# The head of an attention and gated-MLP kernel: one transfer for masks and identity in front, then q and k of the first pair, and half of the filling matmuls

## Chip, cores and metric

One Trainium2 chip, one core. The metric is the device time of one execution in microseconds (us). The kernel before takes 509.92 us (median of 3 runs, 509.29 to 510.59).

## What is computed

Eight batches of 576 tokens. Attention has 8 heads of 64; the first four see a local band of 32 keys, the other four the keys whose position is congruent to the query's modulo 32. Its output, 576 x 512 for a batch, goes through a gated layer with a product over the sequence.

```python
scores = scale * np.matmul(q, k.transpose(0, 1, 3, 2))
mask_local = (rel >= 0) & (rel < stride)
mask_strided = (rel >= 0) & (pos[None, :] % stride == pos[:, None] % stride)
scores = np.where(masks[None, :, :, :], scores, -1000000000.0)
attn = softmax(scores);  x = attn @ v        # heads side by side
h = np.maximum(x @ w_in, 0.0)                # 512 -> 1024
u, v = h[..., :512], h[..., 512:]
v_n = (v - mean(v)) / np.sqrt(var(v) + 1e-06)
v_s = np.einsum('ts,bsd->btd', w_spatial, v_n) + b_spatial[None, :, None]
return ((u * v_s) @ w_out).astype(np.float32)
```

## The kernel before

Heads are worked on in pairs: a batch has two local pairs (`t` modulo 4 is 0 or 1) and two strided ones (2 or 3), 32 pairs in all. A pair is loaded (`q`; `k` of a local pair, or two pieces of `kbd` of a strided one; `v`), its scores are made on TensorE (line 486 local, line 629 strided), maxima, exponentials, sums and a transposition follow on VectorE and ScalarE, the transposed weights are copied into `ptl` or `pts` by ScalarE and GpSimd (lines 391 and 393), and TensorE makes the product with v (line 596 local, line 700 strided). The result `x` (line 413 and 401) feeds the products with w_in (lines 961 and 1018), the product over the sequence (line 1099) and the one with w_out (line 1149). Weights come in blocks by DMA as well and are converted on the way (`convert`, lines 781 to 797), in the first 50 us.

No engine's order is written by hand. Every step is added to a `Program` with a key, a cost for each engine that may do it, and what it reads and writes; `Program.order` simulates the engines and takes from what is ready the step with the smallest key; `Program.emit` issues the steps in that order. All transfers are issued by SyncE (lines 420 and 1290 for loads, 1180 for results), in one queue, the keys of the first ones being `KEYS["la"]`, `KEYS["lb"]`, `KEYS["cst"]` and such. The pairs of the first batch are worked on in the order 0, 2, 1, 3: in the rows below, "the first pair" is `t` = 0 (local), "the third" `t` = 2 (strided), "the second" `t` = 1 (local), "the fourth" `t` = 3 (strided).

For the first four pairs the mask is put into PSUM by TensorE ahead of the scores (`mask_scores`, line 460): minus the identity times minus the mask. Both come by DMA (`cst`, three masks of 64 columns, line 1290; `eye`, the identity, line 1292, into a buffer of the ring of outputs), and ScalarE multiplies them by -1 (lines 1294, 1299 and 1300).

Where TensorE would stand idle in the simulation, `Program.fillers` puts matmuls of zeros ahead of a step: into the PSUM bank that the step is going to overwrite, 256 columns each, as many as fit into a share of the gap (`WARM_SHARE`; line 1378 issues them):

```python
gap = at - max([free, 600.0, *(ends[m] + 200.0 for m in before)])
if gap > WARM_GAP:
    found[n] = int(WARM_SHARE * gap / WARM_COST)
```

Of the kernel before, what the change touches and what calls it, by code (L numbers as in the profile page):

```python
# [9 lines left out]
F32 = mybir.dt.float32  # L10
# [8 lines left out]
B, H, S, D = 8, 8, 576, 64  # L19
# [15 lines left out]
SP = S + STRIDE - RA  # L35
NU = 2 * SB
HS = S // 2
TAIL = S - 4 * P
NT = 4
KEYS = {  # L40
    "a": (-4467.57, -3072.23, -4097.95, -922.09, -62.58, 1948.86, -54.07, 1313.94,),
# [18 lines left out]
    "la": (-2830.09, -2292.21, -5019.65, -1683.98, -4639.4, -3037.2, 298.54, 1600.86,),  # L60
    "lb": (-1002.76, 2105.75, -428.93, 3194.59, 1811.71, 608.19, -588.14, 3548.95,),
}
WARM_END, WARM_GAP, WARM_COST, WARM_COLS, WARM_SHARE = 110000.0, 700.0, 427.0, 256, 0.8
PE_MASKED, APART = (0, 1, 2, 3), ()
OTHER_BANK = (1, 2, 3)
FETCHED, FETCH_COST = 100.0, 32.0
DMA_RATE, DMA_ISSUE, DMA_LAG, DMA_TAIL = 405.0, 475.0, 1600.0, 900.0
# [10 lines left out]
PE, ACT, DVE, POOL, DMA = "tensor", "scalar", "vector", "gpsimd", "sync"  # L78
# [69 lines left out]
class Program:  # L148
# [2 lines left out]

    def __init__(self):
        self.ops, self.writer, self.readers, self.spare = [], {}, {}, {}
        self.tiled, self.port, self.kind = {}, {}, {}

    def add(self, key, choices, fn, reads=(), writes=(), spare=None, tiled=0, port=(), kind=0):


        n = len(self.ops)
        if port:  # L160
            self.port[n] = port
        self.kind[n] = kind
        if spare is not None:
            self.spare[n] = spare
        if tiled:
            self.tiled[n] = tiled
        deps = set()
        for tok in reads:
            if tok in self.writer:
                deps.add(self.writer[tok])  # L170
            self.readers.setdefault(tok, []).append(n)
        for tok in writes:
            if tok in self.writer:
                deps.add(self.writer[tok])
# [139 lines left out]
    def emit(self, nc, warm):  # L314
        issued = self.order()
        fillers = self.fillers(issued)
        for _, n, e in issued:
            if e == PE and fillers.get(n):
                warm(self.spare[n][1], fillers[n])
            self.ops[n][2](getattr(nc, e))  # L320
# [8 lines left out]


@with_exitstack
def attention_moe(ctx, tc, qT, kT, ks, vl, vs, cst, eye, w_in, w_out, wsp, wtail, out):
    nc = tc.nc
    nb = qT.shape[0]

    sb = ctx.enter_context(tc.tile_pool(name="sb", bufs=1))
    ps = ctx.enter_context(tc.tile_pool(name="ps", bufs=1, space=PSUM))
    prog = Program()
    add = prog.add
# [1 line left out]
    def f32(t):  # L341
        return t.bitcast(F32)

    cst_sb = sb.tile([P, 3, 2 * STRIDE], F32, name="cst_sb")
    mask_l0, mask_l, mask_s = cst_sb[:, 0], cst_sb[:, 1], cst_sb[:, 2, :RA]
    w_in_sb = sb.tile([P, 2, NT, DFF], F32R, name="w_in_sb")
    wsp_sb = sb.tile([P, 2, NT, S], F32R, name="wsp_sb")
    wt_h = sb.tile([P, S], F32R, name="wt_h")
# [23 lines left out]
    r_wo = Ring(sb, "w_out", [P, 2, 2, len(BLOCKS), DM // 2], F32R, 1)  # L372
    r_bn = Ring(sb, "bn", [P, 12], F32, 3)
    r_o = Ring(sb, "o", [P, HS], F32, 4)
    at_raw, at_minus = r_o.new(), r_o.new()
    minus = lambda: at_minus()[:, :P].bitcast(F32R)
    masks = lambda i, k: at_minus()[:, P + 2 * STRIDE * i : P + 2 * STRIDE * i + k].bitcast(F32R)
    r_ps = Ring(ps, "s", [P, 512], F32, 2)
# [37 lines left out]

        add(key, [(e, cost[e]) for e in engs], fn, reads, writes)

    def load(key, dst, src, writes, nbytes, reads=()):
        add(key, [(DMA, nbytes / DMA_RATE)], lambda eng: eng.dma_start(dst(), src), reads, writes)  # L420

    xs = {}

# [298 lines left out]
    def attention(t, due):  # L722
        b, hp = divmod(t, NHP)
        local = hp < 2
        q, k = r_q.new(), None
        if t == 2:
            place = r_xt.new()
            v = lambda: f32(place()).rearrange("p a b c -> p (a b c)").rearrange("p (u d) -> p u d", d=D)
        else:
            v = place = r_v.new()  # L730
        fetch_k, fetch_v = (KEYS[n][t] if t < len(KEYS[n]) else due - d for n, d in (("la", 33), ("lb", 20)))
        load(fetch_k - 1, q, qT[b, hp], [(q,)], P * SP * 4)
        if local:
            k = r_k.new()
            load(fetch_k, k, kT[b, hp], [(k,)], P * (STRIDE + S) * 4)
            load(fetch_v, lambda: v()[:, : 2 * LB, :], vl[b, hp], [(place,)], P * 768 * 4)
            kin = [(k,)]
        else:
            for j in range(2):
                load(  # L740
                    fetch_k, lambda j=j: kbd[j::2, t % 2, j, STRIDE:],
                    ks[b, hp - 2, j], [("k", t % 2, j)], 64 * S * 4, [("k0", t % 2)],
                )
            load(fetch_v, v, vs[b, hp - 2], [(place,)], P * 1024 * 4)
            kin = [("k", t % 2, j) for j in range(2)]
        (local_attention if local else strided_attention)(t, due, q, k, v, [(place,)], kin)
# [291 lines left out]
    def keep_tails(bs, key):  # L1038
        xt = r_xt.new()
        xtl[bs[0]] = xt  # L1040
        for i, b in enumerate(bs):
            for hp in range(NHP):
                t = NHP * b + hp
                rnd(
                    key, 2 * TAIL,
                    lambda hp=hp, i=i: xt()[:, hp, :, TAIL * i : TAIL * i + TAIL],
                    lambda t=t: f32(xs[t]())[:, :, 4 * P :],
# [213 lines left out]
    lead = min(nb, 2)  # L1261
# [23 lines left out]
    if nb <= lead:  # L1285
# [1 line left out]
    when, units = zip(*knots)  # L1287
    when = [w - KEYS["lead"][0] for w in when]

    add(KEYS["cst"][0], [(DMA, 330)], lambda eng: eng.dma_start(cst_sb, cst), (), [("cst",)])  # L1290

    load(KEYS["cst"][0] + 1, lambda: at_raw()[:, :P], eye, [(at_raw,)], P * P * 4)
    add(
        KEYS["cst"][0] + 2, [(ACT, 200)], lambda eng: eng.mul(minus(), at_raw()[:, :P], -1.0),
        [(at_raw,)], [(at_minus,)],
    )

    def turn_masks(eng):
        eng.mul(masks(0, 4 * STRIDE), cst_sb[:, :2].rearrange("p a k -> p (a k)"), -1.0)
        eng.mul(masks(2, RA), mask_s, -1.0)  # L1300

    add(
# [84 lines left out]
def _layout(q, k, v, w_in, w_spatial, b_spatial, w_out):  # L1387
    nb = q.shape[0]
    r_major = np.arange(S).reshape(RA, STRIDE).T.reshape(-1)

    def heads(x, width, first):
        xt = np.concatenate([x[:, : H // 2], x[:, H // 2 :][:, :, r_major]], axis=1)
        out = np.zeros((nb, NHP, P, width), np.float32)
        out[..., first : first + S] = xt.transpose(0, 1, 3, 2).reshape(nb, NHP, P, S)
        strided = out[:, NHP // 2 :].reshape(nb, NHP // 2, 2, D, width)
        out[:, NHP // 2 :] = strided.transpose(0, 1, 3, 2, 4).reshape(nb, NHP // 2, P, width)
        return out

    qT, kT = heads(q, SP, 0), heads(k, STRIDE + S, STRIDE)
    ks = kT[:, NHP // 2 :, :, STRIDE:].reshape(nb, NHP // 2, D, 2, S).transpose(0, 1, 3, 2, 4)  # L1400
    vpad = np.zeros((nb, H // 2, S + 32, D), np.float32)
    vpad[:, :, 32:] = v[:, : H // 2]
    vl = np.stack([vpad[:, :, LQ * c : LQ * c + LK] for c in range(LB)], axis=2)
    vl = vl.reshape(nb, 2, 2, LB, LK, D).transpose(0, 1, 4, 3, 2, 5)
    vl = np.ascontiguousarray(vl).reshape(nb, 2, P, 2 * LB, D)
    vsp = v[:, H // 2 :][:, :, r_major].reshape(nb, 2, 2, STRIDE, RA, D)
    vsp = vsp[:, :, :, [[strided_residue(c, i) for i in range(4)] for c in range(SB)]]
    vs = np.zeros((nb, 2, 4, STRIDE, SB, 2, D), np.float32)
    vs[:, :, :, :RA] = vsp.transpose(0, 1, 4, 5, 3, 2, 6)
    vs = vs.reshape(nb, 2, P, NU, D)  # L1410

    cst = np.zeros((P, 3, 2 * STRIDE), np.float32)
    i = np.arange(STRIDE)[:, None]
    j = np.arange(2 * STRIDE)[None, :]
    band = np.where((j > i) & (j <= i + STRIDE), 0.0, NEG)
    cst[:, :2] = np.tile(band, (4, 1))[:, None]
    cst[:STRIDE, 0] += np.where(j < STRIDE, NEG, 0.0)
    cst[:, 2] = np.tile(np.where((j > i) & (i < RA), NEG, 0.0), (4, 1))

    def words(w):  # L1420
        w = np.ascontiguousarray(w)
        return w.view(np.int64) if w.dtype == np.float64 else w

    wspT = np.ascontiguousarray(w_spatial.T)
    wtail = np.zeros((2, P, S), np.float32)
    wtail[0, :TAIL] = wspT[4 * P :]
    wtail[0, TAIL:] = wspT[4 * P :]
    wtail[1, :TAIL] = wspT[4 * P :]
    wtail[1, TAIL] = wtail[1, 96] = b_spatial
    return {  # L1430
        "qT": qT,
        "kT": np.ascontiguousarray(kT[:, : NHP // 2]),
        "ks": np.ascontiguousarray(ks),
        "vl": vl,
        "vs": vs,
        "cst": cst,
        "eye": np.eye(P, dtype=np.float32),
        "w_in": words(w_in.reshape(NT, P, 2, HF).transpose(0, 2, 1, 3)),
        "w_out": words(w_out),
        "wsp": wspT[: 4 * P],  # L1440
        "wtail": wtail,
    }
# [19 lines left out]
```

## Time and profile before

| | |
|---|---|
| median of 3 runs | 509.92 us (509.29 to 510.59) |
| the profiled execution | 509.85 us, of it span 507.8 us |
| TensorE (PE) busy | 495.6 us, 98% of the span |
| VectorE (DVE), ScalarE (ACT), GpSimd (POOL) busy | 344.7, 280.3, 111.7 us |
| DMA | 52.71 MB, 104 GB/s on average |
| mean granted TensorE clock | 0.99 of full speed |

A matmul in float32 shows up as two records. The profile calls weight loads PEld and the sync queue's issues SPq. "Granted clock" is the share of full speed (2.4 GHz) that TensorE was given; a DMA's time to landing counts from the start of its issue. The chain of waits follows back from the last instruction what released each step.

### The profile page before, as it was taken

What the parts mean: (1) busy time and instruction counts of PE and PEld (TensorE: products, weight loads), DVE (VectorE), ACT (ScalarE), POOL (GpSimd) and SP (SyncE); (2) the same over time, 40 slices, a digit from 0 to 9 for tenths busy, and PEclk for the clock granted to TensorE, in tenths of its full rate; (3) what the DMA queues carried; (4) which work ended last, traced back from release to release, by engine and by line L of the source; (5) the groups of instructions that cost most, each with busy time, mean ns of one, the idle gap of its engine ahead of it and who ended that gap; (6) DMA issues with size and microseconds to landing.
All of it is one profiled execution on the core that took longest, in us unless ns stands there. A gap on an engine that the chain in (4) does not pass through costs nothing.

```text
span 507.8 us, 15733 instructions
## 1 busy us (share of the span) xinstructions
PE 495.6 (98%) x6398; PEld 455.2 (90%) x6398; DVE 344.7 (68%) x1069; ACT 280.3 (55%) x871; POOL 111.7 (22%) x229
## 2 busy tenths in 40 slices
PE   7599999999999999999999999999999999999997
PEld 4478898889988999899998999989998899989997
DVE  3988898988678628784488925687288841666055
ACT  5897777577546556373654765355554642235214
POOL 3553426133232013020221211121022200120000
PEclk9699999999999999999999999999999999999999
DMA  8996443422423412204224243024131020002002
GB/s 288 397 359 222 125 139 108 137 93 64 144 92 119 127 50 91 90 25 151 81 92 138 76 132 89 4 90 139 60 99 45 1 94 0 1 2 93 1 1 94
DMA packets 26247, 52.71 MB, mean 104 GB/s; under 512 B 3136, under 2 KB 11584, under 8 KB 26176
## 3 DMA queue, kind: packets, MB, share of 16 engines
q1 hardware_dynamic: 26176, 51.72, 31.0%
q8 instruction: 50, 0.82, 0.7%
q14 instruction: 21, 0.17, 0.1%
HBM read 42.27 MB, written 9.44 MB: 102 GB/s over the span
## 4 chain that ended last, share of the span: by engine, by line
PE 95%; DMA 4%; SPq 0%; issue 0%; ACT 0%
PE m L961 21%; PE m L1018 20%; PE m L1099 20%; PE m L1149 18%; PE po L700 3%; PE po L596 3%; DMA q<-qT 3%; PE s L486 2%; PE s L629 2%; PE m L1111 2%; PE m L1112 2%; DMA kbd<-ks 1%; PE po L1378 0%; SPq L420 0%; PE m L629 0%
## 5 line engine op out<-in xcount | busy, mean ns | idle before, releaser
L1099 PE MATMUL m<-wsp_sb,vn 128*128 128x288 f32 x768 | 112.9, 296 | 0.0
L1099 PEld LDWEIGHTS m<-wsp_sb,vn 128*128 128x128 f32 x768 | 105.5, 189 | 0.9
L1018 PE MATMUL m<-x,w_in_sb 128*128 128x288 f32 x768 | 105.3, 297 | 0.0
L1018 PEld LDWEIGHTS m<-x,w_in_sb 128*128 128x128 f32 x768 | 103.0, 188 | 0.6
L961 PE MATMUL m<-w_in_sb,x 128*128 128x512 f32 (+1 forms) x408 | 99.4, 398 | 0.0
L1149 PE MATMUL m<-g,w_out 128*128 128x288 f32 x672 | 92.9, 296 | 0.0
L1149 PEld LDWEIGHTS m<-g,w_out 128*128 128x128 f32 x672 | 89.9, 188 | 1.3
L961 PEld LDWEIGHTS m<-w_in_sb,x 128*128 128x128 f32 (+1 forms) x408 | 74.1, 185 | 18.3
L393 POOL TENSOR_SCALAR ptl<-pc 32x64 f32<-32x64 f32 (+3 forms) x98 | 38.5, 393 | 105.5 <-DVE pc L567 69.5
L916 DVE BATCH_NORM_STATS2 bn<-vv 128x6 f32<-128x512 f32 (+1 forms) x37 | 25.2, 683 | 47.4 <-ACT vv L911 47.1
L391 ACT CAST g<-u 128x288 fp32r<-128x288 f32 x91 | 39.0, 435 | 29.4 <-DVE u L812 13.1
L543 ACT ACTIVATE pl<-pl,ml 128x64 f32<-128x64 f32 (+1 forms) x140 | 47.0, 337 | 7.9 <-DVE ml L523 7.8
L929 POOL TENSOR_TENSOR bn<-bn,sel 128x1 f32<-128x1 f32 (+1 forms) x37 | 21.5, 582 | 130.0 <-DVE bn L924 125.2
L401 DVE TENSOR_TENSOR g<-u,g 128x288 fp32r<-128x288 f32 x98 | 43.6, 459 | 7.5 <-ACT g L391 5.2
L911 ACT ACTIVATE vv<-m 128x512 f32<-128x512 f32 (+1 forms) x37 | 21.9, 596 | 47.0 <-PE m L961 46.7
L1032 ACT ACTIVATE u<-m 128x288 f32<-128x288 f32 x56 | 22.9, 409 | 41.2 <-PE m L1018 40.5
L1121 DVE TENSOR_TENSOR u<-m,u 128x288 f32<-128x288 f32 x56 | 24.9, 453 | 30.5 <-PE m L1112 29.9
L391 ACT COPY ptl<-pc 32x320 f32<-32x320 f32 (+3 forms) x94 | 33.5, 356 | 13.7 <-DVE pc L567 11.9
L413 ACT CAST x<-po 128x288 fp32r<-128x288 f32 x60 | 22.1, 399 | 22.2 <-PE po L700 10.3
L401 DVE TENSOR_TENSOR x<-po,x 128x288 fp32r<-128x288 f32 x64 | 27.3, 447 | 8.4 <-ACT x L413 7.9
L523 DVE CUSTOM_DVE_ANT_0 pl<-s,cst_sb 128x64 f32<-128x64 f32 (+1 forms) x140 | 22.1, 215 | 14.5 <-PE s L486 14.5
L543 ACT ACTIVATION_READ_ACCUMULATOR pl<-pl,ml 128x1 f32 (+1 forms) x140 | 26.3, 188 | 0.0
(128 smaller groups left out, 632.8 us busy)
## 6 DMA issues: line engine op xcount, KB each, us to landing
q<-qT SPq DMA_DIRECT2D x32, 295.0 KB, 4.3
v_raw<-vs SPq DMA_DIRECT2D x15, 512.0 KB, 3.8
v_raw<-vl SPq DMA_DIRECT2D x16, 384.0 KB, 3.7
k<-kT SPq DMA_DIRECT2D x16, 304.0 KB, 4.5
kbd<-ks SPq DMA_DIRECT2D x32, 144.0 KB, 4.9
outT<-o SPq DMA_DIRECT2D x32, 144.0 KB, 1.9
outT<-u SPq DMA_DIRECT2D x28, 144.0 KB, 1.8
vn<-w_in SPq DMA_DIRECT2D x4, 512.0 KB, 7.5
```

Source lines behind the costliest of these rows:

```text
L391: eng.copy(dst(), src())
L393: eng.tensor_scalar(dst(), src(), 1.0, 0.0, op0=ALU.mult, op1=ALU.add)
L401: eng.tensor_tensor(dst(), src(), f32(hi()), op=ALU.subtract)
L413: eng.copy(dst(), src())
L543: eng.activation(p_sb()[:m, u, :], src, AF.Exp, bias=st()[:m, u : u + 1], scale=SCALE if masked else -1.0, **total,)
L916: lambda eng: eng.bn_stats(bn()[:m, 0:6], v()[:m]), [(v,)], [(bn,)],
L961: eng.matmul(v_ps()[:m, :], x_at(kt)[:, a, :], w_in_sb[:, w, kt, HF:], start=(n == 0 and i == 0), stop=(n == NT - 1 and i == 2),)
L1018: eng.matmul(u_ps()[:, :HS], w_in_sb[:, w, kt, f * P : (f + 1) * P], xs[NHP * b + kt]()[:, a, r], start=(n == 0 and i == 0), stop=(n == NT ...
L1032: lambda eng, u=u, f=f, u_ps=u_ps: eng.activation(flat(u)[:, f * HS : (f + 1) * HS], u_ps()[:, :HS], AF.Relu),
L1099: eng.matmul(s_ps()[:, :HS], vn()[:, a, kt, fs], wsp_sb[:, w, kt, r], start=(kt == 0 and i == 0), stop=False,)
L1121: lambda eng, ug=ug, s_ps=s_ps: eng.tensor_tensor(ug(), s_ps()[:, :HS], ug(), op=ALU.mult),
L1149: eng.matmul(o_ps()[:, :HS], w_out_t[0]()[:, w, r, BLOCKS[name], j * P : (j + 1) * P], at(a), start=(first and r == 0 and i == 0), stop=(r ...
```

## The change

- The masks and the identity lie side by side in one array `cst` of 274 columns (137 KB), `cst_sb` holds it, and one DMA brings it; `eye`, its DMA and its buffer are gone. The step of the identity remains in the program as one that issues nothing.
- Steps can have a `lead`; `emit` issues those ahead of everything else, in the order of their numbers: `cst` (0), q of the first pair (1), k of the first pair (2). The simulated order is made without regard to it.
- `WARM_SHARE` is 0.4 instead of 0.8.

```diff
-WARM_END, WARM_GAP, WARM_COST, WARM_COLS, WARM_SHARE = 110000.0, 700.0, 427.0, 256, 0.8
+WARM_END, WARM_GAP, WARM_COST, WARM_COLS, WARM_SHARE = 110000.0, 700.0, 427.0, 256, 0.4
...
+        if lead is not None:
+            self.lead[n] = lead
...
     def emit(self, nc, warm):
         issued = self.order()
         fillers = self.fillers(issued)
+        for n in sorted(self.lead, key=self.lead.get):
+            self.ops[n][2](getattr(nc, DMA))
         for _, n, e in issued:
+            if n in self.lead:
+                continue
...
-    cst_sb = sb.tile([P, 3, 2 * STRIDE], F32, name="cst_sb")
-    mask_l0, mask_l, mask_s = cst_sb[:, 0], cst_sb[:, 1], cst_sb[:, 2, :RA]
+    cst_sb = sb.tile([P, CST], F32, name="cst_sb")
+    mask_l0, mask_l = cst_sb[:, : 2 * STRIDE], cst_sb[:, 2 * STRIDE : 4 * STRIDE]
+    mask_s, one = cst_sb[:, 4 * STRIDE : 4 * STRIDE + RA], cst_sb[:, CST - P :]
...
-        load(fetch_k - 1, q, qT[b, hp], [(q,)], P * SP * 4)
+        load(fetch_k - 1, q, qT[b, hp], [(q,)], P * SP * 4, lead={0: 1}.get(t))
...
-            load(fetch_k, k, kT[b, hp], [(k,)], P * (STRIDE + S) * 4)
+            load(fetch_k, k, kT[b, hp], [(k,)], P * (STRIDE + S) * 4, lead={0: 2}.get(t))
...
-    add(KEYS["cst"][0], [(DMA, 330)], lambda eng: eng.dma_start(cst_sb, cst), (), [("cst",)])
-    load(KEYS["cst"][0] + 1, lambda: at_raw()[:, :P], eye, [(at_raw,)], P * P * 4)
+    add(KEYS["cst"][0], [(DMA, 330)], lambda eng: eng.dma_start(cst_sb, cst), (), [("cst",)], lead=0)
+    add(KEYS["cst"][0] + 1, [(DMA, P * P * 4 / DMA_RATE)], lambda eng: None, (), [("one",)])
     add(
-        KEYS["cst"][0] + 2, [(ACT, 200)], lambda eng: eng.mul(minus(), at_raw()[:, :P], -1.0),
-        [(at_raw,)], [(at_minus,)],
+        KEYS["cst"][0] + 2, [(ACT, 200)], lambda eng: eng.mul(minus(), one, -1.0),
+        [("one",)], [(at_minus,)],
     )
```

How the instructions stand now. On VectorE, ScalarE and GpSimd every instruction keeps its place; on the other two, the rows below are all that differs. First the sync queue at the start of the program, before:

```order
L420 DMA q_1_83<-qT 128x590
L1290 DMA cst_sb_61<-cst 128x192
L420 DMA o_0_91<-eye 128x128
L420 DMA q_0_97<-qT 128x590
L420 DMA k_0_100<-kT 128x608
L420 DMA vn_0_103<-w_in 128x1024
L420 DMA kbd_68<-ks 64x576 x2
```

and now (`q_0` and `k_0` are the first pair's, `q_1` the third's, `vn_0` holds the first block of w_in):

```order
L1301 DMA cst_sb_61<-cst 128x274
L429 DMA q_0_82<-qT 128x590
L429 DMA k_0_84<-kT 128x608
L429 DMA q_1_88<-qT 128x590
L429 DMA vn_0_101<-w_in 128x1024
L429 DMA kbd_68<-ks 64x576 x2
```

The masks moved from second to first, the first pair's q and k from fourth and fifth to second and third, the third pair's q from first to fourth; all that follows stands one place further ahead. Then TensorE, where the filling matmuls stand (those of `zeros`), before:

```order
L1378 MATMUL s_0_116<-zeros_67 32x256 x8
L460 MATMUL s_0_116<-o_1_110 128x64
...
L1378 MATMUL po_0_337<-zeros_67 32x256
L596 MATMUL po_0_337<-ptl_72,v_raw_0_182 64x96 x6
...
L1378 MATMUL po_4_524<-zeros_67 32x256 x3
L596 MATMUL po_4_524<-ptl_72,v_raw_1_276 64x96 x6
```

and now:

```order
L1388 MATMUL s_0_114<-zeros_67 32x256 x4
L471 MATMUL s_0_114<-o_1_108 128x64
...
L497 MATMUL m_2_132<-k_1_106,q_2_184 32x64
L607 MATMUL po_0_331<-ptl_72,v_raw_0_176 64x96 x6
...
L1388 MATMUL po_4_517<-zeros_67 32x256
L607 MATMUL po_4_517<-ptl_72,v_raw_1_270 64x96 x6
```

There are 4 instead of 8 ahead of the first masks, none instead of 1 ahead of the first pair's product with v (it follows the second pair's scores directly), and 1 instead of 3 ahead of the second pair's product, which is the third that TensorE makes.

## Rows read from the trace of the kernel before

**Rows 1.** The page: TensorE's busy time, share of the span and instructions; and the shares of the chain that ended last, by engine.

```profile
PE 495.6 (98%) x6398; PEld 455.2 (90%) x6398; DVE 344.7 (68%) x1069; ACT 280.3 (55%) x871; POOL 111.7 (22%) x229
PE 95%; DMA 4%; SPq 0%; issue 0%; ACT 0%
```

**Rows 2.** The chain that ended last, in order of time, of the first 45 us: start, duration (us), what.

```profile
2.10 4.90 DMA q<-qT
...
7.09 5.88 DMA kbd<-ks
...
13.63 8.03 DMA q<-qT
...
21.80 1.17 PE m L629 x64
...
25.80 5.10 PE m L961 x21
30.89 1.41 PE po L1378 x6
```

**Rows 3.** The timeline of the sync queue: start of the issue, its duration (us), line, transfer.

```profile
0.72 0.39 SPq L420 DMA_DIRECT2D q<-qT  x1
1.16 0.42 SPq L1290 DMA_DIRECT2D cst_sb<-cst  x1
1.63 0.42 SPq L420 DMA_DIRECT2D o<-eye  x1
2.10 0.43 SPq L420 DMA_DIRECT2D q<-qT  x1
2.57 0.43 SPq L420 DMA_DIRECT2D k<-kT  x1
7.09 1.16 SPq L420 DMA_DIRECT2D kbd<-ks  x2
10.57 0.33 SPq L420 DMA_DIRECT2D q<-qT  x1
```

**Rows 4.** The DMA issues, asked for at the times 1.16, 1.63, 2.10, 2.57, 10.57 and 13.63, one each: transfer, KB, us from issue to landing.

```profile
cst_sb<-cst SPq DMA_DIRECT2D x1, 96.0 KB, 2.7
...
o<-eye SPq DMA_DIRECT2D x1, 64.0 KB, 3.1
...
q<-qT SPq DMA_DIRECT2D x1, 295.0 KB, 4.9
...
k<-kT SPq DMA_DIRECT2D x1, 304.0 KB, 5.2
...
q<-qT SPq DMA_DIRECT2D x1, 295.0 KB, 6.5
...
q<-qT SPq DMA_DIRECT2D x1, 295.0 KB, 8.0
```

**Rows 5.** Stretches of the first 6 us: from and to, length, busy time (and instructions) of each engine, granted clock, DMA share, GB/s.

```profile
2.50:3.00 0.50, 0.50 (x2) 0.18 (x1) 0.50 (x1) 0.50 (x1) 0.50 (x2) 1.00 0.99 376
3.00:5.00 2.00, 2.00 (x6) 0.89 (x5) 0.05 (x1) 1.39 (x5) 0.52 (x2) 1.00 0.77 156
5.00:5.50 0.50, 0.50 (x2) 0.18 (x1) 0.00 (x0) 0.07 (x1) 0.00 (x0) 1.00 1.05 373
```

**Rows 6.** The timeline of TensorE, weight loads of the first fillers among it: start, duration (us), engine, line, what, count, and the idle time before with what ended it.

```profile
0.94 6.00 PE L1378 MATMUL s<-zeros 128*32 128x256 f32 x16 [0.94 <-DVE zeros L1332]
1.79 0.18 PEld L1378 LDWEIGHTS s<-zeros 128*32 128x32 f32 x1 [0.25 <-issue]
8.26 0.97 PE L486 MATMUL s<-k,q 64*32 64x64 f32 x72
9.92 0.76 PE L629 MATMUL m<-kbd,q 128*32 128x36 f32 x64 [0.69 <-DMA k<-kT]
17.08 1.34 PE L486 MATMUL m<-k,q 64*32 64x64 f32 x72 [6.39 <-DMA q<-qT]
18.35 1.06 PE L1378 MATMUL po<-zeros 128*32 128x256 f32 x2
19.34 2.19 PE L596 MATMUL po<-ptl,v_raw 128*64 128x96 f32 x24
32.23 1.28 PE L596 MATMUL po<-ptl,v_raw 128*64 128x96 f32 x24
```

**Rows 7.** Stretches around the change of the granted clock, columns as in rows 5 (PE first, the clock third from the end).

```profile
13.00:17.00 4.00, 0.00 (x0) 0.00 (x0) 3.96 (x10) 2.63 (x8) 0.40 (x2) 0.50 1.02 393
17.00:22.00 5.00, 4.65 (x112) 3.41 (x116) 3.93 (x9) 4.24 (x12) 4.32 (x9) 0.50 1.03 405
23.00:24.00 1.00, 1.00 (x17) 0.59 (x19) 0.97 (x4) 1.00 (x9) 1.00 (x2) 1.00 1.06 393
22.96:25.80 2.84, 2.27 (x70) 1.70 (x68) 2.46 (x5) 2.23 (x16) 1.86 (x3) 1.00 1.04 396
```

**Rows 8.** The timeline of ScalarE at the masks, and of TensorE's weight loads where they waited for `ptl`.

```profile
3.86 0.31 ACT L1299 ACTIVATE o<-cst_sb 128x128 fp32r<-128x128 f32 x1
4.76 0.31 ACT L1294 ACTIVATE o<-o 128x128 fp32r<-128x128 f32 x1 [0.48 <-DMA o<-eye]
...
19.34 1.90 PEld L596 LDWEIGHTS po<-ptl,v_raw 128*64 128x64 f32 x24 [0.81 <-POOL ptl L393]
...
32.23 1.09 PEld L596 LDWEIGHTS po<-ptl,v_raw 128*64 128x64 f32 x24 [0.41 <-POOL ptl L393]
```

More of the change, by code (lines that the diff above doesn't have):

```diff
@@ L38 @@
 TAIL = S - 4 * P
+CST = 4 * STRIDE + RA + P
 NT = 4
@@ L153, in __init__, with add @@
         self.ops, self.writer, self.readers, self.spare = [], {}, {}, {}
-        self.tiled, self.port, self.kind = {}, {}, {}
-    def add(self, key, choices, fn, reads=(), writes=(), spare=None, tiled=0, port=(), kind=0):
+        self.tiled, self.port, self.kind, self.lead = {}, {}, {}, {}
+    def add(self, key, choices, fn, reads=(), writes=(), spare=None, tiled=0, port=(), kind=0, lead=None):
         n = len(self.ops)
@@ L331, in attention_moe @@
 @with_exitstack
-def attention_moe(ctx, tc, qT, kT, ks, vl, vs, cst, eye, w_in, w_out, wsp, wtail, out):
+def attention_moe(ctx, tc, qT, kT, ks, vl, vs, cst, w_in, w_out, wsp, wtail, out):
     nc = tc.nc
@@ L374, in attention_moe @@
     r_o = Ring(sb, "o", [P, HS], F32, 4)
-    at_raw, at_minus = r_o.new(), r_o.new()
+    at_minus = r_o.new(skip=(0,))
     minus = lambda: at_minus()[:, :P].bitcast(F32R)
@@ L417, in evac, with load @@
         add(key, [(e, cost[e]) for e in engs], fn, reads, writes)
-    def load(key, dst, src, writes, nbytes, reads=()):
-        add(key, [(DMA, nbytes / DMA_RATE)], lambda eng: eng.dma_start(dst(), src), reads, writes)
+    def load(key, dst, src, writes, nbytes, reads=(), lead=None):
+        add(
+            key, [(DMA, nbytes / DMA_RATE)], lambda eng: eng.dma_start(dst(), src), reads, writes,
+            lead=lead,
+        )
     xs = {}
@@ L1288, in attention_moe @@
     when = [w - KEYS["lead"][0] for w in when]
-    add(KEYS["cst"][0], [(DMA, 330)], lambda eng: eng.dma_start(cst_sb, cst), (), [("cst",)])
-    load(KEYS["cst"][0] + 1, lambda: at_raw()[:, :P], eye, [(at_raw,)], P * P * 4)
-    add(
-        KEYS["cst"][0] + 2, [(ACT, 200)], lambda eng: eng.mul(minus(), at_raw()[:, :P], -1.0),
-        [(at_raw,)], [(at_minus,)],
+    add(KEYS["cst"][0], [(DMA, 330)], lambda eng: eng.dma_start(cst_sb, cst), (), [("cst",)], lead=0)
+    add(KEYS["cst"][0] + 1, [(DMA, P * P * 4 / DMA_RATE)], lambda eng: None, (), [("one",)])
+    add(
+        KEYS["cst"][0] + 2, [(ACT, 200)], lambda eng: eng.mul(minus(), one, -1.0),
+        [("one",)], [(at_minus,)],
     )
     def turn_masks(eng):
-        eng.mul(masks(0, 4 * STRIDE), cst_sb[:, :2].rearrange("p a k -> p (a k)"), -1.0)
+        eng.mul(masks(0, 4 * STRIDE), cst_sb[:, : 4 * STRIDE], -1.0)
         eng.mul(masks(2, RA), mask_s, -1.0)
@@ L1410, in _layout @@
     vs = vs.reshape(nb, 2, P, NU, D)
-    cst = np.zeros((P, 3, 2 * STRIDE), np.float32)
     i = np.arange(STRIDE)[:, None]
     j = np.arange(2 * STRIDE)[None, :]
[L1415 to L1418, printed above, removed]
+    band = np.tile(np.where((j > i) & (j <= i + STRIDE), 0.0, NEG), (4, 1))
+    band0 = band.copy()
+    band0[:STRIDE] += np.where(j < STRIDE, NEG, 0.0)
+    causal = np.tile(np.where((j > i) & (i < RA), NEG, 0.0), (4, 1))
+    cst = np.concatenate([band0, band, causal[:, :RA], np.eye(P)], axis=1).astype(np.float32)
     def words(w):
@@ L1436, in _layout @@
         "cst": cst,
-        "eye": np.eye(P, dtype=np.float32),
         "w_in": words(w_in.reshape(NT, P, 2, HF).transpose(0, 2, 1, 3)),
```

## Prediction

> **What bounds the kernel now.** I read the page first: TensorE is busy for 98% of the span, and the chain of waits is 95% TensorE and 4% DMA [rows 1]. Nearly all of the time is dense matmul that this change leaves as it is; only the head of the kernel can move, and what the head gains or loses is carried to the end by the unbroken TensorE chain. The second view is that chain in order of time [rows 2]. The reader is to see transfers in a row: q of the first local pair from 2.10 to 7.00, a piece of `kbd` from 7.09, and q of the fourth pair from 13.63 to 21.66. Only at 21.80 does the chain go over to TensorE.
>
> Why transfers, and why those? The issue times on the sync queue [rows 3] beside the times to landing [rows 4] show it. The first issues are 0.47 us apart. The `kbd` piece issued at 7.09 is the twelfth DMA, and the fourth, q, issued at 2.10, landed 4.9 us later, at 7.00. So eight are in flight, and the next one goes when the one eight places ahead has landed. And the stream runs full: 376 GB/s from 2.5 us, then a thin stretch of 156 GB/s from 3 to 5, 373 from 5 on [rows 5], and 393 to 405 later [rows 7]. The q of the second pair, issued at 10.57, lands 6.5 us later, at 17.07, and TensorE's scores of that pair start at 17.08; the q issued at 13.63 lands 8.0 us later, at 21.6, just ahead of 21.80 [rows 2, 3, 4, 6]. **The head is a full stream of bytes. It gets shorter only if the stream runs full earlier, or if there is less in it.**
>
> **The change part by part.**
>
> *Transfers.* Ahead of the first w_in block stood 295 + 96 + 64 + 295 + 304 = 1054 KB in five issues; now it is 137 + 295 + 304 + 295 = 1031 KB in four. The 23 KB are worth 0.06 us at 400 GB/s. The missing issue moves all that follows forward by one slot of 0.47 us (1.16 to 1.63) [rows 3]. The q of the third pair moves from the first place to the fourth, three slots or 1.4 us; its user stands at 9.92 on TensorE and waits for another transfer there [rows 6], so this costs nothing unless that q is over 4 us later.
>
> What a slot is worth at the far end is bounded from both sides. Below: if the thin stretch from 3 to 5 us stays where it is, whatever is queued, only the 0.06 us are left. Above: if the two small transfers cause it and it is gone, the stream moves 0.8 MB in those 2 us at 400 GB/s instead of 0.31 MB at 156 [rows 5], 0.49 MB or 1.2 us more, with the bytes 1.3 us. I take slot and bytes, 0.47 + 0.06 = **0.5 us**: the thin stretch follows two issues that brought only 160 KB in 0.94 us, which fits a queue short of bytes; but the 64 KB that took 3.1 us, and the q behind them that took 4.9 [rows 4], say that part of it is latency, which the new front transfer has too.
>
> *First filling matmuls, 8 to 4.* The 16 records took 6.0 us, the first ones 0.43 us apart (0.18 load, 0.25 gap) [rows 6], so eight records end at 0.94 + 3.4 = 4.4 us. The mask matmuls behind them then wait for ScalarE. Its three multiplications ran from 3.86 to 5.07, 0.48 us of it waiting for the identity [rows 8]; the one transfer, issued at 0.72, takes 2.7 us if it is like `cst_sb` now [rows 4], and all three are done by about 4.6. The masks run from 4.7 for the time that they take now or somewhat more, and the first scores wait for k, which lands at 2.57 + 5.2 = 7.77 now and, issued 0.94 us earlier, at 6.8: **they start about 1.4 us ahead of the 8.26 of now** [rows 3, 4, 6]. This is not on the path, since TensorE's next steps wait for transfers at 9.92 and 17.08 [rows 6], and those move by 0.5. The 1.4 us become slack on VectorE and ScalarE: worth 0 at the end, and up to 1.4 if the stream were not the bound.
>
> *The one matmul before the first V product, removed.* It took 1.06 us at 18.35, but the product behind it waited 0.81 us for GpSimd's copies into `ptl` [rows 6, 8]. Those hide it. They come at least 0.5 us earlier by the steps above, and without the removal the product could not follow them; no term of its own.
>
> *Three to one before the third product.* 1.41 us in the chain become 0.47 [rows 2]. The product waited another 0.41 us for `ptl` [rows 8], so bare waiting takes the fillers' place: 0 again, and at most 0.94 us of gain if `ptl` came early.
>
> *TensorE's clock.* The rows show 0.50 of full speed, the 1.2 GHz level, from 13 to 22 us, after an engine that did next to nothing from 10.7 to 17.1, and 1.00 again from 23, after it had worked 4.65 of the 5 us from 17 [rows 6, 7]. With the stream 0.5 us earlier and the return at the same time, 0.5 us more of work lies at the lower level. A V product took 2.19 us there and 1.28 at the higher one [rows 6], so 42% of it is lost: 0.2 us. I take **0.15**, since the return may move with the work.
>
> *Sum.* Against the profiled execution, 509.85 us (span 507.8, 2.05 around it; the median of the runs is 509.92, so it is a typical one): 509.85 - 0.5 + 0.15 = **509.5 us**. A measurement of this kernel can tell about 0.3%, 1.5 us, from no change (the three runs lie 1.3 us apart), so this is "no change".
>
> **The rivals.**
>
> *A, slower: the clock returns later.* The matmuls taken away are work without waits. Without the 1.06 us at 18.35 the engine pauses between the second pair's scores, which now end near 17.9, and the V product, and again between that and the q of the fourth pair near 21.1; before, the 5 us from 17 held 0.35 us of pauses [rows 7]. Against it: the first pause closes if `ptl` is 1 us early. Price: if the return slips by 3 us, the 2.27 us of work from 22.96 to 25.80 [rows 7] lie at the lower level; by the V product's ratio they take 71% longer, +1.6 us, and the copies of x behind them pass this on through ScalarE and VectorE to `ptl`. Less 0.5 from the stream: +1.1, **510.9 us**. It decides from a return about 1 us late, where it eats the gain; past 26 us the dense stretch from 25.80 [rows 2] adds 0.5 us for each. The Trainium skill, page "TensorE: Matmul & The Clock Gate", section "Part 1: The HAM clock gate (the "warmup" mystery)", has the rule behind this rival: "the default state is throttled, and activity releases the throttle". By that rule fillers taken away can only delay the return; the fall after the idle stretch and the return after 17 to 22 us agree with it.
>
> *B, a larger gain: the thin stretch closes.* For: it coincides with the two small transfers. Against: the q behind them was slow as well. Price: the stream is 1.3 us ahead; if the clock returns no earlier, 42% of that is lost, 0.55 us (509.1 us), and nothing if it moves along (508.5 us): about **508.8 us**. The Trainium skill, page "DMA: Bandwidth & Descriptors", section "Anatomy of one DMA", gives some 2.0 us plus the bytes at 436 GB/s for a DMA, measured on another issuing path than this kernel's. By it an estimate for q in the second place is 2.7 us instead of the row's 4.9, which favours this rival; the identity's row, 3.1 us against an estimate of 2.15, does not agree with it.
>
> *C, the edit does not reach the bound.* The stream is full from the same moment, and the earlier scores are hidden: -0.06, **509.8 us**. For: the thin stretch may belong to the start and not to what is queued.
>
> **How the numbers follow.** Forecast 0.50 (509.1 to 509.8), B 0.20, C 0.17, A 0.13. To hold 8 in 10 with the measurement's own spread, the range reaches to B's 508.5 and A's 510.9. Faster by over 1.5 us (below 508.4) needs B with something more, such as the 0.94 us of fillers: 0.08. Slower by over 1.5 us (above 511.4) needs A with a return past 26 us: 0.06. The rest, 0.86, is within 0.3%.
>
> **What would show it.** Right: the q of the second pair landing near 16.5 and that of the fourth near 21.1, the first scores near 7, and the dense stretch of w_in products that started at 25.80 starting 0.3 to 0.5 us earlier. B: bandwidth near 400 GB/s from 3 us on, and the fourth pair's q before 20.6. A: granted clock still 0.50 after 23 us. Wrong altogether: a difference that arises after 40 us, where the engines' orders are the same.

## The result and the profile after

The changed kernel takes **512.86 us** (median of 13 runs, 510.66 to 515.38), the kernel before beside it 509.89 (13 runs): ratio 1.0061, 95% interval 1.0047 to 1.0074. It is slower, by about twice what a measurement can tell, and outside the forecast range. The profiled execution took 512.68 us, its span is 510.5. It is one with a low mean clock (0.98); a second profile of the same kernel, *changed again* below, has 0.993 and took 510.66, which is of use: the two show apart what the head and what the rest did. One run of an experiment (e1), at 680 us with a mean granted clock of 0.65, is not counted in its numbers.

The page of the changed kernel: engines, instruction queues, the chain by engine.

```profile
PE 495.2 (97%) x6384; PEld 456.4 (89%) x6384; DVE 346.0 (68%) x1069; ACT 280.0 (55%) x871; POOL 110.8 (22%) x229
...
q8 instruction: 50, 0.82, 0.7%
...
PE 95%; DMA 3%; POOL 1%; issue 0%; ACT 0%; SPq 0%; DVE 0%; POOLq 0%
```

Against [rows 1] TensorE is busy 0.4 us less, in a span that is 2.7 us longer: it waits more. 14 matmuls and 14 weight loads fewer are the seven fillers (two records each): 28 instructions. Queue q8 brings instructions, 16 KB a packet.

The chain in order of time (start, duration) and the timeline of TensorE in the head.

```profile
9.90 7.35 DMA q<-qT
...
21.98 1.19 PE m L640 x64
...
26.62 6.59 PE m L972 x21
```

```profile
0.93 3.62 PE L1388 MATMUL s<-zeros 128*32 128x256 f32 x8 [0.93 <-DVE zeros L1342]
...
6.55 0.97 PE L497 MATMUL s<-k,q 64*32 64x64 f32 x72
```

```profile
17.30 1.34 PE L497 MATMUL m<-k,q 64*32 64x64 f32 x72 [7.00 <-DMA q<-qT]
18.57 2.19 PE L607 MATMUL po<-ptl,v_raw 128*64 128x96 f32 x24
21.98 1.19 PE L640 MATMUL m<-kbd,q 128*32 128x36 f32 x64 [1.22 <-DVE ml L525]
...
26.55 6.66 PE L972 MATMUL m<-w_in_sb,x 128*128 128x512 f32 x21
33.13 0.62 PE L1388 MATMUL po<-zeros 128*32 128x256 f32 x2
33.68 1.21 PE L607 MATMUL po<-ptl,v_raw 128*64 128x96 f32 x24
```

Against [rows 2, 6]: the first scores are 1.71 us earlier, the second pair's 0.22 later, the dense stretch starts 0.8 us later and takes 6.59 us instead of 5.10 in the chain, and the V product behind it is 1.45 late (32.23 to 33.68). The clock is why: stretches of the same profile, columns as in [rows 5].

```profile
3.00:5.00 2.00, 2.00 (x6) 0.87 (x5) 0.05 (x1) 1.25 (x5) 0.52 (x2) 1.00 0.95 319
...
17.00:22.00 5.00, 3.48 (x100) 3.05 (x101) 3.97 (x11) 4.21 (x14) 3.89 (x8) 0.50 1.04 405
...
24.00:29.00 5.00, 5.00 (x72) 3.79 (x72) 3.78 (x10) 2.75 (x11) 2.07 (x3) 0.50 1.03 404
29.00:30.00 1.00, 1.00 (x4) 0.78 (x3) 1.00 (x3) 1.00 (x3) 0.00 (x0) 0.56 1.02 392
```

It is at 0.50, the 1.2 GHz level, until almost 30 us; before, it was back by 23 [rows 7]. From 17 to 22 TensorE worked 3.48 of 5 us instead of 4.65. (The thin stretch of transfers from 3 to 5 us has gone from 156 to 319 GB/s.)

But of the 2.7 us only 1.1 are there when the scores at 54 us of the kernel before start. The rest comes at two places where both kernels issue the same work. The changed kernel at 89 and at 269 us:

```profile
88.18 0.72 PE L607 MATMUL po<-ptl,v_raw 128*64 128x96 f32 x12
88.82 0.77 PE L640 MATMUL s<-kbd,q 128*32 128x36 f32 x64
89.53 0.72 PE L607 MATMUL po<-ptl,v_raw 128*64 128x96 f32 x12
90.17 0.62 PE L640 MATMUL s<-kbd,q 128*32 128x36 f32 x46
91.20 0.38 PE L640 MATMUL s<-kbd,q 128*32 128x36 f32 x18 [0.40 <-issue]
...
268.54 0.74 PE L640 MATMUL s<-kbd,q 128*32 128x36 f32 x60
269.94 0.26 PE L640 MATMUL s<-kbd,q 128*32 128x36 f32 x4 [0.65 <-issue]
```

The kernel before, the same work, without a break:

```profile
85.81 1.33 PE L961 MATMUL m<-w_in_sb,x 128*128 128x512 f32 x5
87.06 0.72 PE L596 MATMUL po<-ptl,v_raw 128*64 128x96 f32 x12
87.71 0.77 PE L629 MATMUL s<-kbd,q 128*32 128x36 f32 x64
88.41 0.72 PE L596 MATMUL po<-ptl,v_raw 128*64 128x96 f32 x12
89.06 0.77 PE L629 MATMUL s<-kbd,q 128*32 128x36 f32 x64
...
266.72 0.77 PE L629 MATMUL s<-kbd,q 128*32 128x36 f32 x64
```

"issue" is a wait for nothing that the profile shows. How late a step is against the profile of the kernel before is the difference of its start times in the two timelines; for the scores that start there at 82, 107, 254 and 290 us it is +1.11, +1.74, +1.77, +2.69: two steps, 0.63 and 0.92, one at each pause and each about 0.25 us more than the idle time in its row. So 1.1 of the 2.7 us come out of the head, where the clock is late, and 1.55 from the two pauses.

### The profile page after: what moved, and what is told of

Same layout as the page of the kernel before. It is cut to its first block, busy times and chain, and to the rows that moved or that the text cites. A ratio compares the mean times of both kernels' runs of the same rounds, so it can differ in the third digit from the quotient of the medians.

```text
span 510.5 us, 15704 instructions
## 1 busy us (share of the span) xinstructions
PE 495.2 (97%) x6384; PEld 456.4 (89%) x6384; DVE 346.0 (68%) x1069; ACT 280.0 (55%) x871; POOL 110.8 (22%) x229
## 4 chain that ended last, share of the span: by engine, by line
PE 95%; DMA 3%; POOL 1%; issue 0%; ACT 0%; SPq 0%; DVE 0%; POOLq 0%
PE m L972 21%; PE m L1029 20%; PE m L1110 20%; PE m L1160 18%; PE po L607 4%; PE po L711 4%; PE s L497 2%; PE s L640 2%; PE m L1122 2%; PE m L1123 2%; DMA q<-qT 1%; DMA k<-kT 1%; PE m L497 0%; PE m L640 0%; POOL kbd L1324 0%
## 5 line engine op out<-in xcount | busy, mean ns | idle before, releaser
L972 PE MATMUL m<-w_in_sb,x 128*128 128x512 f32 (+1 forms) x408 | 101.6, 404 | 0.0
L972 PEld LDWEIGHTS m<-w_in_sb,x 128*128 128x128 f32 (+1 forms) x408 | 75.6, 189 | 18.8
```

What stands on the lines that cost most here:

```text
L972: eng.matmul(v_ps()[:m, :], x_at(kt)[:, a, :], w_in_sb[:, w, kt, HF:], start=(n == 0 and i == 0), stop=(n == NT - 1 and i == 2),)
```

## Experiments

Theory S (**stream**): TensorE's instructions arrive in blocks, and 28 fewer in the head move every later block end against the work, so that at two places a block is used up before the next arrives. Rivals: K (**clock**), the fillers taken away let the clock stay low; T (**transfers**), the new front or the order of q and k costs. Small matmuls put in behind the first fillers (32 columns, 4 instructions each) change the stream's length and little else:

```diff
+        for _ in range(PADS.pop(0) if PADS else 0):
+            nc.tensor.matmul(buf()[:STRIDE, :STRIDE], zeros, zeros, start=True, stop=True)
```

Fillers are written as three numbers, those at the three places: 8, 1, 3 before, 4, 0, 1 changed.

| kernel | fillers | stream against before | median us | ratio, 95% interval |
|---|---|---|---|---|
| e1 transfers only | 8, 1, 3 | 0 | 509.86 | 0.9989 (0.9975 to 1.0002) |
| e2 fewer fillers only | 4, 0, 1 | -28 | 512.33 | 1.0050 (1.0030 to 1.0071) |
| e3 changed + 28 | 4, 0, 1 | 0 | 509.42 | 0.9982 (0.9968 to 0.9995) |
| e4 changed, middle filler back | 4, 1, 1 | 0 | 509.10 | 0.9982 (0.9970 to 0.9994) |
| e5 before, wider fillers | 3, 1, 1 | -28 | 511.77 | 1.0045 (1.0024 to 1.0065) |
| e6 changed + 8 | 4, 0, 1 | -20 | 509.90 | 1.0006 (0.9985 to 1.0027) |
| e7 changed + 56 | 4, 0, 1 | +28 | 509.83 | 0.9992 (0.9979 to 1.0005) |
| e8 middle filler back, short | 4, 1, 1 | -24 | 510.15 | 0.9995 (0.9983 to 1.0007) |
| e9 middle filler back, + 56 | 4, 1, 1 | +28 | 509.04 | 0.9980 (0.9968 to 0.9991) |
| e10 before, no middle filler | 8, 0, 3 | 0 | 509.86 | 1.0001 (0.9987 to 1.0014) |
| e12 masks first only | 8, 1, 3 | 0 | 509.73 | 0.9999 (0.9985 to 1.0013) |
| c1 changed again | 4, 0, 1 | -28 | 511.76 | 1.0030 (1.0012 to 1.0049) |
| e13 changed + 28 late | 4, 0, 1 | -28, then 0 | 511.18 | 1.0026 (1.0003 to 1.0048) |

The kernel before took 509.80 us beside e1 to e4, 510.01 beside e5 to e8, 509.83 beside e9 to c1, 509.97 beside e13.

**The two halves of the change.** e1 keeps the transfers, e2 the fillers:

```diff
-WARM_END, WARM_GAP, WARM_COST, WARM_COLS, WARM_SHARE = 110000.0, 700.0, 427.0, 256, 0.4
+WARM_END, WARM_GAP, WARM_COST, WARM_COLS, WARM_SHARE = 110000.0, 700.0, 427.0, 256, 0.8
```

(e1, on the changed kernel; e2 is the reverse, on the kernel before.)

> The changed kernel with the filling matmuls of before (8, 1 and 3; share 0.8): the transfer part alone. TensorE's instruction stream has the length of before. If the fillers are the cause (the clock at 1.2 GHz until 29.5 us instead of 22.6, +1.1 us at 50 us, and two pauses of TensorE that the profile calls issue, near 91 and 270 us, +0.64 and +0.88 us), this is at 509.4 to 510.0, with the clock back near 22 to 23 us and no pause at 91 and 270. If the new order of the transfers is the cause, it stays at 512 to 513.

> The kernel before with share 0.4 (4, 0 and 1 filling matmuls): the filler part alone; TensorE's instructions are 28 fewer, as in the changed kernel. Fillers as cause: 512 to 513.5, clock late, pauses at 91 and 270 us. Transfers as cause: 510, as before.

The whole loss comes with the fillers: e1 is 0.1% faster than before if anything, e2 0.5% slower. In e2's profile the clock is back early (0.78 from 20 to 22 us, 1.00 from 22), which was not expected; its scores at 82 us are 0.12 us ahead, at 107 us 0.79 late, at 290 us 1.73 late. T falls, and K does not explain e2's steps.

**The stream's length.** e3 and e4 restore it, 7 small matmuls with the fillers 4, 0, 1, and 6 with 4, 1, 1:

> The changed kernel with 28 TensorE instructions put back behind the first fillers, as seven matmuls of 32 columns of zeros (some 50 ns each record), so that every later instruction has the number in the stream that it has in the kernel before. If the pauses at 91 and 270 us come from where the stream's blocks of 256 instructions end, they are gone, the 0.57 us pause of before at 24 us comes back, and the time is 0.9 to 1.5 us less than the changed kernel's: 511.4 to 512. If they come from other things (clock, transfers), they stay and so does the time, 512.9.

> As the previous kernel, but with the one filling matmul ahead of the first V product put back (4, 1 and 1; the stream kept at the length of before by six small matmuls instead of seven). If the pause of TensorE between 20.8 and 22.0, or between scores and V product, keeps the clock low, and this filler bridges it: clock back near 22 to 23 us, about 510.2. If the early ones matter (8 against 4) or the clock's return is a matter of phase: as the previous kernel, 511.4 to 512.

Both are faster than the kernel before, neither has a pause at 89 or 267 us, and the middle filler makes no difference in the ratio. That the pauses go was forecast; the times were not: e3 is 2 us below its 511.4 to 512 and has no pause at 24 us, e4 is 1.1 us below its 510.2. e5 asks the reverse: the kernel before, with wider but fewer fillers (1536 columns instead of 2048 in the first ones, 512 instead of 768 in the last), so that the stream is 28 instructions shorter:

```diff
-        for _ in range(count):
+        for cols in {8: (512, 512, 512), 1: (256,), 3: (512,)}[count]:
             nc.tensor.matmul(
-                buf()[:STRIDE, :WARM_COLS], zeros,
+                buf()[:STRIDE, :cols], zeros,
```

> The kernel before, its fillers written with fewer instructions: three matmuls of 512 columns for the eight of 256, the middle one as it is, one of 512 for the three. Order and transfers are those of before; from the first V product on, every TensorE instruction has the number in the stream that it has in the changed kernel (28 less). If the place of the instructions in the stream costs the time: pauses near 91 and 270 us as in the changed kernel, clock as in before (0.989 to 0.993), and 512 to 512.4 us. If only fewer fillers and a slower clock cost it: 509.8 to 510, without those pauses.

It is slower by 0.45% (511.77, just under what was expected), with the old transfers, the middle filler in place, a clock of 0.993 in its profile and of 0.987 or more in 11 of its 12 runs, so that neither T nor K can be the cause. TensorE's timeline has the breaks of the changed kernel, behind the same 46th and 60th record:

```profile
88.51 0.62 PE L629 MATMUL s<-kbd,q 128*32 128x36 f32 x46
89.95 0.39 PE L629 MATMUL s<-kbd,q 128*32 128x36 f32 x18 [0.82 <-issue]
...
267.36 0.74 PE L629 MATMUL s<-kbd,q 128*32 128x36 f32 x60
268.99 0.26 PE L629 MATMUL s<-kbd,q 128*32 128x36 f32 x4 [0.89 <-issue]
```

**The place of the block's end.** e6, e7 and e8 put in 2, 14 and no small matmuls:

> The changed kernel with 8 instructions put back (two matmuls of 32 columns) instead of 28. By the place in the stream, the pause near 91 us falls 4 of 64 records earlier in its run of scores and most of both pauses stays: 512 to 512.8. If the small matmuls help in another way (as work ahead of the masks), about as with 28: 509.5 to 510.5.

> The changed kernel with 56 instructions more (14 matmuls of 32 columns): every later instruction is as far behind its place in the kernel before as it was ahead of it in the changed kernel. By the place in the stream, no block of 256 begins with the two runs of scores near 88 and 267 us any more, so no pauses there: 509 to 510, unless another run is hit. If a stream shorter or longer than that of before is bad as such: 511 or more.

> The changed kernel with the middle filler put back (4, 1, 1) and nothing else: four instructions more than the changed kernel, 24 fewer than before. The clock as with the middle filler (0.989 to 0.993), the pauses near 91 and 270 us as in the changed kernel. If both causes count on their own: 511.2 to 511.8, between the changed kernel (512.9) and the one with middle filler and full stream (509.1). If the clock is all: 509.1 to 509.5. If the place is all: 512.5 to 513.

e6, the timeline of TensorE:

```profile
89.96 0.59 PE L642 MATMUL s<-kbd,q 128*32 128x36 f32 x42
91.71 0.40 PE L642 MATMUL s<-kbd,q 128*32 128x36 f32 x22 [1.16 <-issue]
...
268.96 0.77 PE L642 MATMUL s<-kbd,q 128*32 128x36 f32 x64
```

e8, the weight loads at the same run (its matmuls, whose ends are modelled, show no gap):

```profile
87.64 0.49 PEld L644 LDWEIGHTS s<-kbd,q 128*32 128x32 f32 x44
88.37 0.27 PEld L644 LDWEIGHTS s<-kbd,q 128*32 128x32 f32 x20 [0.24 <-issue]
```

The break stands behind record 46, 44 and 42 for streams 28, 24 and 20 shorter than before: two instructions a record, so always at the same instruction, number 3,010 counted in the order of TensorE's program. The second one stands at 7,874, and one in the head of the kernel before, behind the 19th of 64 records of line 700, at 706. They lie 9 x 256 and 19 x 256 instructions apart. That is the block. The place is exact; the length is not: 0.40, 0.82, 1.16 and 0.24 us at the first, and e6, which should still have the second, shows none there (what decides this is worked out under the step that failed). e7 has neither pause, in spite of a low clock (0.982 in its profile), and its time was as expected. The times of e6 and e8 were not: e6's 509.90 lies 2 us below the 512 to 512.8 that its place in the stream was to cost and in the range of its rival (against which e5 and e13 speak), e8's 510.15 in none of its three ranges. In e6 one of the two pauses is missing, and in e8 both are small: +0.35 us between the scores at 82 and 107 us, +0.21 between those at 254 and 290.

**Behind the head.** All those instructions were put in at the head, where they might do something else as well. e13 puts seven small matmuls in at 179 us, between the two runs of scores:

```diff
+            if e == PE and n in self.spare and LATE[0] and at > LATE[0]:
+                late, LATE[0] = self.spare[n][1], 0
+                warm(late, -7)
```

> The changed kernel with seven small matmuls (28 instructions) put in behind its head, between the pauses at 91 and 270 us. If the place of a run of score matmuls in TensorE's instruction stream sets its pause: the run at 91 us has its place of the changed kernel, so its pause stays (1.0 to 1.4 us between the scores at 82 and at 107 us), and the run at 270 us has its place of the kernel before, so its pause goes (under 0.2 us between the scores at 254 and at 290 us, instead of 0.9). Time 0.6 to 0.9 us below the changed kernel, 510.9 to 512.0, ratio 1.002 to 1.004. If the fewer fillers of the head slow the later scores in another way (the clock, the transfers, TensorE's lead over the other engines), both pauses stay and the time is 511.8 to 513.

```profile
91.40 0.62 PE L644 MATMUL s<-kbd,q 128*32 128x36 f32 x46
92.70 0.38 PE L644 MATMUL s<-kbd,q 128*32 128x36 f32 x18 [0.68 <-issue]
...
270.44 0.77 PE L644 MATMUL s<-kbd,q 128*32 128x36 f32 x64
```

The first pause stays, the second is gone: +0.90 us between the scores at 82 and 107 us, -0.01 between those at 254 and 290. Its step was 0.92 in the changed kernel. So the pauses come from the place in the stream, and not from anything else that the head does: theory S is shown for them. The time is within what was expected but tells little by itself: the seven matmuls cost 0.5 us (the lag grows by that much between the scores at 125 and at 176 us), and its interval includes c1's ratio.

**The rest: clock, transfers, and the changed kernel again.**

> The kernel before, with the one filling matmul before the first V product taken out and one small matmul put in behind the first fillers, so that the stream has as many instructions as before. If that filler holds TensorE's clock, about a third of the runs show a mean granted clock of .983 or less, and the median is 0.3 to 0.6 us higher, 510.2 to 510.6; the pauses at 91 and 270 us must not appear. If the clock's spread has another cause (the four first fillers, the transfers), the clocks are .989 and over and the time is that of before, 509.9.

> The changed kernel with the filling matmul before the first V product back (4, 1, 1) and 13 small matmuls behind the first fillers, so that TensorE's stream is 28 instructions longer than before (12,981). If block ends in the stream set the pauses, a longer stream moves them out of the runs of score matmuls at 91 and 270 us as the 28 more of the changed kernel did: no pause of over 0.3 us released by issue there, and with the clock held by the middle filler 508.9 to 509.5 us, ratio about 0.998. If instead the loss of the changed kernel came with the transfers in front or with the four first fillers, this one keeps both and stays above 511.

e10 is half a miss. Without the filler of 1.06 us ahead of the first V product the mean granted clock is lower: .983 in 2 of 12 runs and .985 to .987 in 6, against none below .987 in the 103 runs of the kernel before beside e1 to e12. Its profile, columns as in [rows 5]:

```profile
17.00:22.00 5.00, 3.66 (x111) 3.23 (x114) 4.40 (x11) 4.65 (x15) 4.09 (x9) 0.50 1.04 401
...
23.00:25.00 2.00, 2.00 (x23) 1.25 (x27) 1.93 (x4) 1.19 (x9) 0.96 (x3) 0.50 1.04 400
```

So that filler does hold the clock. But the median did not move, 509.86 against 509.83; the price of 0.3 to 0.6 us was not seen. e9, with the filler, had .989 to .993 in all 12 runs and is the best of the thirteen, if by no more than the intervals of e3 and e4.

e12 has the new front transfer, but q and k of the first pair in their old places:

```diff
-        load(fetch_k - 1, q, qT[b, hp], [(q,)], P * SP * 4, lead={0: 1}.get(t))
+        load(fetch_k - 1, q, qT[b, hp], [(q,)], P * SP * 4)
```

(and the same for `k`, on e1).

> Masks and identity as one transfer in front, but q and k of the first local pair left where they were in the queue, and all fillers as before (8, 1, 3). If the gain of the transfers comes from the one issue less (0.47 us for all that follows), this one has it too: 509.4 to 509.6, ratio 0.999. If it comes from k of the first pair standing earlier, this one is at 509.9 like the kernel before. No pauses at 91 and 270 us by either, since the stream has as many instructions as before.

The time decides nothing (0.9999, its interval includes e1's 0.9989). The landings do say something: q of the second and fourth pair land at 16.62 and 21.22, 0.41 and 0.44 us earlier than before; that is about the slot.

> The changed kernel once more, with nothing else, beside the three others on the same chip. If its loss belongs to the kernel and not to a chip or a day: 512.3 to 513.2, ratio 1.005 to 1.007, with pauses released by issue in the runs of score matmuls at 91 and 270 us. If the loss was of that chip: 509.5 to 510.5.

```profile
16.54 1.34 PE L497 MATMUL m<-k,q 64*32 64x64 f32 x72 [6.63 <-DMA q<-qT]
...
21.23 0.76 PE L640 MATMUL m<-kbd,q 128*32 128x36 f32 x64 [1.23 <-DMA q<-qT]
...
24.53 5.16 PE L972 MATMUL m<-w_in_sb,x 128*128 128x512 f32 x21
```

```profile
89.37 0.38 PE L640 MATMUL s<-kbd,q 128*32 128x36 f32 x18 [0.91 <-issue]
...
268.05 0.26 PE L640 MATMUL s<-kbd,q 128*32 128x36 f32 x4 [0.65 <-issue]
```

Slower again, by 0.3%: less than in the first measurement, and less than expected. In this profile the clock was back by 22 us, and everything is to be seen apart: 1.22 us ahead at 82 us, then +1.13 at the first pause and +0.87 at the second, +0.8 at the end. The profile of the first measurement has the same two steps (0.63 and 0.92) and the late clock besides. Low clocks were commoner there, .983 or less in 10 of 13 runs against 5 of 12 here, which fits the larger ratio; that they make up all of the difference was not tested. Within c1 itself, the four runs at 0.993 or more took 510.29 to 510.68 us, the five at .983 or less 511.94 to 514.76.

## Why the prediction was wrong

**The step that failed** is the first filling matmuls "8 to 4", and with it the two other fillers, costed at 0 because other work hides them *where they stand*. Apart from the clock they do cost nothing there. But an instruction taken out of TensorE's program shifts all that follow against the 256-instruction blocks in which they arrive, and the prediction did not ask for that. What the runs showed in place of the 0 is two pauses of TensorE, at 91 and 270 us, that cost 1.55 us in the first profile and 2.0 us in c1's. A second term was too small: the clock, taken at +0.15 us, cost some 2 us in the runs in which it came back late, and in the first measurement most did. The prediction named the sign of the first itself: "a difference that arises after 40 us, where the engines' orders are the same".

How 28 instructions turn into a pause can be worked out from the rows. The block that ends ahead of instruction 3,010 begins at 2,754. In the changed kernel it holds the last third of the V product at 88.18 (9 instructions, 0.2 us), the first run of scores (128; 0.71 us to the next step), the other half of the V product (27; 0.64) and 92 of the second run (0.5): TensorE is through in some 2.1 us. In the kernel before it begins 28 instructions earlier in the work: 10 instructions of dense products, 5 records of 0.25 us, then 0.65, 0.70, 0.65 and half a run of scores, 0.35: 3.6 us. Against this stands what a block takes to come. The packet of q8 ahead of the pause, a DMA view of the changed kernel from 88.7 to 88.9 us:

```profile
q8 instruction: 1, 0.02, 29.6%
```

The matmul behind the pause starts at 91.20, 2.4 us after it; at 269.94 it is 2.3 us, in the pauses of the other runs 2.3 to 2.8. In none of the fifteen profiles, at 735 block ends in all, does a block's first instruction start less than 2.29 us after the block's packet began to move. Here the packet moves at 88.85, after TensorE has begun the block ahead of it, and that block is used up in 2.1 us: TensorE has to wait. In the kernel before the packet moved at 84.28, ahead of the whole block and 5.0 us before it was needed.

The second place shows that it is the packet that decides. The block that ends ahead of 7,874 is used up in some 2.2 us in both kernels, and the one before does not pause. The kernel before and the changed one, the runs in which this block begins (at 264.92 and 266.82), and the packets, seen from 263.8 to 264.0 and from 267.5 to 267.7:

```profile
264.85 0.77 PE L629 MATMUL s<-kbd,q 128*32 128x36 f32 x64
q8 instruction: 1, 0.02, 31.6%
...
266.63 0.77 PE L640 MATMUL s<-kbd,q 128*32 128x36 f32 x64
q8 instruction: 1, 0.02, 30.3%
```

The packet moved at 263.88, 1.0 us ahead of the block's first instruction, in the one, and at 267.62, 0.8 us behind it, in the other. In e6 it moved 0.2 us ahead (267.03), and there is no pause; at the first place 1.16 us behind, and its pause is the longest; in e8 0.06 us behind, and its pause is the shortest. What sets the moment of the packet was not tested.

The Trainium skill, page "Runtime: NRT & Kernel Launch", section "Instruction fetch mechanics", states the blocks of 256 instructions that the counts above show, and says of crossing a block's end that its cost is "mostly hidden". For most of the fifty block ends of a kernel that holds here; at two of the changed kernel, and at a third in c1 (0.35 us, at 706), it does not. In c1 the two turn a head that is 1.22 us ahead into a kernel that is 0.8 us slower.

The trace of before had a sign of it: the chain held an "issue" of 0.57 us in the middle of a run of small matmuls, at 24.32 us, ahead of the x45 of line 700. I passed it over.

**Size.** e5, with nothing but the stream changed in length (and some columns of zeros), costs 0.45%, 2.3 us (1.8 us by the medians). The changed kernel against e3, which only restores the length, is 0.8% slower by the ratio of the first measurement and 0.5% by c1's; low clocks, which were rarer in e3, are part of that.

**Transfers, -0.5.** The mechanism was right. In c1 the q's land at 16.49 and 21.09, forecast 16.5 and 21.1. In the first profile they landed at 17.25 and 21.84 although issued 0.67 and 0.84 us earlier, at 9.90 and 12.79 instead of 10.57 and 13.63: [rows 4]'s 6.5 and 8.0 us to landing became 7.4 and 9.1. e1 measures -0.56 us for this part alone (-1.3 to +0.1), which does not set it apart from no change. The dense stretch came earlier than forecast: at 24.53 in c1 and 24.22 in e1, 1.2 and 1.5 us ahead of before, not 0.3 to 0.5; in c1 the clock was back earlier too (0.72 on average from 17 to 22 us, against 0.50).

Rival B's thin stretch did close for the most part (156 to 319 GB/s), yet the landings did not gain more than the slot.

**First scores, near 7:** 6.55, and as forecast they are slack. **The fillers before the V products:** in the first profile the first product did not wait for `ptl` at all, the third waited 0.41 us for it as before [rows 8]; in c1, where it came earlier, it waited 0.66 us. The bare wait takes the fillers' place, as costed. What the prediction did not see on this path: in the first profile the scores of the fourth pair waited at 21.98 for VectorE's `ml`, not for their q.

**The clock, +0.15, and rival A (0.13).** The mechanism of A was right for the first profile, and its 0.5 us for a microsecond past 26 too: the dense x21, with 3.3 us of it at the lower level, took 1.5 us more. The whole was dearer in A than on the chip: with the return after 29 us A gives 1.6 + 0.5 x 3.5 - 0.5 = 2.9 us, and the lag at the V product was 1.45 (0.82 where the x21 starts, 1.49 more in it, less 0.86 for the fillers removed behind it). And the middle filler is what A said it was: in the seven profiles that have it the clock is back between 19.5 and 22.8 us, in the eight without it between 19.8 and 29.9.

But a late clock does not come in every run (.983 or less in 10 of 13 of the first measurement, 5 of 12 in c1, 7 of 24 in e3 and e7). Where it comes it costs some 2 us: in e3, which has no pauses, the five runs at 0.993 took 508.09 to 509.31 us and the three at 0.982 509.89 to 510.39. Too few of e3's runs had it to move its ratio, the same 0.9982 as that of e4 with the middle filler; in the first measurement most had it, and its median of 512.86 holds the late clock and the pauses together. A alone does not reach it: e5, whose clock is that of before, loses its 0.45% to the pauses, and A's own 510.9 falls 2 us short. Why low clocks were so much commoner in the first measurement than in e3 stays open.

## What to carry to other kernels

In this kernel, an instruction removed or added early was not local: it moved every later block of the instruction stream of the engine that is the bound. Look in the timeline for waits on "issue" within runs of small matmuls, and where 256 instructions take only some 2.4 us expect that an edit ahead of them can make or end a pause; compare versions at several stream lengths before you credit the edit itself. The edit as meant was good, if by little: with its stream brought back to the old length it is 0.2% faster than the kernel before (e3; e4 with the middle filler), not 0.6% slower, and with 28 instructions more than that (e7) it cannot be told from it.

## What the runs showed of the hardware that was not expected

A block's packet comes late where the queues are full of loads. In e13, with the loads at 409 GB/s from 20 to 25 us and 405 from 25 to 30, the packet of the block that begins at 706 moved only at 24.56, 6.1 us after TensorE had begun the block ahead of it, and TensorE stood still for 2.5 us in the run of line 715, which up to there is the same program as in c1 (0.35 us) and in the first profile (no pause):

```profile
23.85 0.66 PE L715 MATMUL po<-pts,xt 64*64 64x36 f32 x29
27.05 0.77 PE L715 MATMUL po<-pts,xt 64*64 64x36 f32 x35 [2.54 <-issue]
```

In all fifteen profiles this packet moved 3.2 us or more after the block ahead had begun, against 2.2 us ahead to 1.2 us behind for the blocks at 3,010 and 7,874, where the loads are thinner (181 GB/s from 84 to 90 us and 63 from 262 to 268 in the kernel before). That the full queues are the reason was not tested. Behind the long pause the granted clock fell again, to 0.71 on average from 29 to 34 us, and the dense x21 took 6.72 us instead of c1's 5.16. It is one more source of the spread of these runs (509.2 to 514.7 us in e13).
